# Every second block inverse of a chunked recurrence worked out on GpSimd

## The chip, the cores and the metric

The kernel runs on one core of a Trainium2 chip. A core has five engines, which take their own instructions in order and wait for each other by semaphores: TensorE (PE, matrix products; its weight loads are listed as PEld), VectorE (DVE), ScalarE (ACT), GpSimd (POOL) and SyncE (SP, which here only issues DMAs). DMAs are issued by SP and by POOL, from the same in-order queues as the other instructions of these engines. The metric is the device time of one launch in microseconds (us).

## The reference

Two parts follow each other. The first is a recurrence with a 40 x 40 state for each of 4 x 8 heads over 768 steps; the second a two-layer MLP on its output.

```python
for t in range(S):                                   # S = 768
    y[:, :, t] = np.einsum('bhd,bhde->bhe', rt, state)
    Sa = np.einsum('bhde,bhe->bhd', state, at)
    state_decay = state * wt[:, :, None, :] - np.einsum('bhd,bhe->bhde', Sa, bt)
    state = state_decay + np.einsum('bhd,bhe->bhde', vt, kt)
...
x = attn_out.transpose(0, 2, 1, 3).reshape(B * S, H * D)   # 3072 x 320
h = x @ w_in                                         # 320 -> 2048
sp = np.where(h > 20.0, h, np.log1p(np.exp(np.minimum(h, 20.0))))
g = h * np.tanh(sp)
out = g @ w_out                                      # 2048 -> 320
```

## The kernel before

**The recurrence in chunks.** The 768 steps are cut into 12 chunks of 64, taken in six pairs. In a chunk, the steps act on each other through a strictly lower triangular matrix, and the inverse of identity plus that matrix turns 64 dependent steps into matrix products. For each chunk there are four pieces of work.

- `pre_a(c, be)` (L126 to L203, twice for each chunk): the loads of `wa` and `bk` on SP's queue; the running products P of the decays by scans on DVE (L145 to L157), of which the last columns are copied out at L150; `bk` scaled on DVE (L170); P stored to `pD` from POOL's queue (L172); products on PE (L186) that give the triangular blocks `GP` and the factor `HA`, evicted by ACT (L188 to L190) and DVE (L191, L193); a small memset on POOL (L198) and transposes on PE (L202) for `bkn`.
- `pre_inv(n)` (L205 to L221, once for each pair): all 32 x 32 diagonal blocks of the pair are inverted at once, one block in a partition. DVE transposes `GP` into the tile `XL` (L209) and sets its diagonal to one (L210). Then 30 steps of forward substitution: step i multiplies column i below the diagonal with the first i elements of row i into `tmp` (L214) and adds that to `XL` (L216). Both have (31-i)*i elements in a partition, 30 to 240. There is one buffer for `XL` and one for `tmp`, and each of the 60 operations needs the one before. L218 transposes `XL` into `TT`, L220 part of that into `T1` (kept in `GP`'s tile).
- `post_inv(n)` (L223 to L260): PE multiplies with `TT` (L232), ACT evicts (L235), PE multiplies with `T1` (L241), ACT gathers the blocks of the 64 x 64 inverse in `bdT` (L249 to L251), and PE forms with them and `HA` the matrix `KT` of each chunk of the pair (L258, evicted at L260).
- `step(c)`: what hangs on the state. PE multiplies `KT` with `VS` (L284), evicted into `UVT` (L286), transposed (L293) into `UVQ`, multiplied with `bdr` (L314, masked on DVE at L316), and L334 and L339 give the output, which ACT evicts into `yev` (L343), and the next state, which DVE makes (L342, L346) and PE transposes (L304). The loads of the next chunk into `VS` (L267), `UVT` (L270) and `bdr` (L271), single buffers each, and the store of `yev` to `yD` (L370) stand on POOL's queue.

The loop over pairs goes: step 2n, `pre_a` of pair n+2, inverse of pair n+1, step 2n+1. The inverses n = 1, 3 and 5 are those of the second, fourth and sixth pair; steps 2, 6 and 10 need them.

**The MLP.** The weights come as 64-bit values and are turned into two float32 parts in pieces of 512 columns. A piece takes a DMA (`cv_d`, on SP's queue), an ACT operation (L459), three on DVE (L461 to L463), one on ACT (L494) and one on DVE (L495), with single buffers for most of the pieces. They are issued beside the last pairs of the recurrence. The matmuls of the first layer (L585) and the second (L605 to L607) follow; they read `yD` and `pD` back.

**What sets the order.** The code is written in loops; a scheduler orders the instructions of each engine by priorities, to which a table of offsets (`OFF`) adds for each part. What stands first in an engine's queue is waited for.

Of the kernel before, what the change touches and what calls it, by code (L numbers as in the profile page):

```python
# [10 lines left out]
ALU = mybir.AluOpType  # L11
# [67 lines left out]
def attention(ctx, tc, I, yD, pD, nch, M):  # L79
    nc = tc.nc  # L80
    V, A, PE, SP, G = nc.vector, nc.scalar, nc.tensor, nc.sync, nc.gpsimd
# [123 lines left out]
    def pre_inv(n):  # L205
        gp = GP[n]

        X = iw.tile([128, 32, 32], F32, name="XL", bufs=NXL)
        V.transpose(X.rearrange("p t j -> p j t"), gp[:, :, 1].rearrange("p u j -> p j u"))  # L209
        V.memset(X.rearrange("p t j -> p (t j)")[:, 0:1024:33], 1.0)  # L210
        for i in range(1, 31):
            tmp = iw.tile([128, 240], F32, name="tmp", bufs=NTMP)
            tv = tmp[:, 0:(31 - i) * i].rearrange("p (t j) -> p t j", j=i)
            V.tensor_tensor(out=tv, in0=X[:, i + 1:32, i:i + 1].broadcast_to([128, 31 - i, i]),  # L214
                            in1=X[:, i:i + 1, 0:i].broadcast_to([128, 31 - i, i]), op=ALU.mult)
            V.tensor_tensor(out=X[:, i + 1:32, 0:i], in0=X[:, i + 1:32, 0:i], in1=tv, op=ALU.add)  # L216
        TT = iw.tile([128, 32, 32], F32, name="TT", bufs=NTT)
        V.transpose(TT.rearrange("p u t -> p t u"), X)  # L218
        T1 = gp[0:64, :, 0]
        V.transpose(T1, TT[0:64])  # L220
        return TT, T1  # L221
# [159 lines left out]
    def inv(n):  # L381
        with at(tc, 'I%d' % n), at(tc, 'I'):
            TT, T1 = pre_inv(n)
        with at(tc, 'J%d' % n):
            post_inv(n, TT, T1)
# [274 lines left out]
```

## Time and profile before

| | |
|---|---|
| median of 3 runs | 845.22 us (842.81 to 847.49) |
| the profiled execution | 842.54 us |
| its span in the profile | 840.7 us |
| recurrence, up to about | 470 us |
| PE busy over the span | 737.5 us (88%) |
| DVE busy | 463.3 us (55%) |
| ACT busy | 427.9 us (51%) |
| POOL busy | 103.3 us (12%) |
| DMA | 61.92 MB, 74 GB/s over the span |

The busy rows average over stages. The profile also cuts the span in 40 slices of 21 us; each digit is the busy share in tenths:

```profile
PE   2545898998989889888749999999999999999998
...
DVE  6789889659879758947962649221222222122110
ACT  4533657774665766676457646333333333333331
POOL 8100021132123023211210200000000000000000
PEclk9755699899999999999978999999999999999999
```

For the first 22 slices PE, DVE and ACT share the work of the recurrence; behind them PE is full. POOL does little but issue DMAs after its memsets at the start. What lies around the span in the execution is 1.84 us.

### The profile page before, as it was taken

Reading aid. Unit: us, or ns where it says so; the run is one execution under the profiler, and the core shown is the slowest. Engines: PE = TensorE matmul, PEld = TensorE weight load, DVE = VectorE, ACT = ScalarE, POOL = GpSimd, SP = SyncE. Lnnn points to the kernel's source line nnn. Section 1 sums busy time; section 2 is a strip of 40 time slices with the busy share of each in tenths; the row PEclk is TensorE's granted clock in tenths of the full one; section 3 lists DMA queues with packets and bytes.
Section 4 is the critical chain, followed back from the end, with each engine's and each line's share of the span. In section 5 each row is a group of like instructions: output and inputs, shape, how many; then the busy total and the mean of one; then the engine's idle time right before and its main releaser. Section 6 shows DMA issues by size and latency. Waiting matters only on the chain.

```text
span 840.7 us, 18817 instructions
## 1 busy us (share of the span) xinstructions
PE 737.5 (88%) x7816; PEld 688.5 (82%) x7816; DVE 463.3 (55%) x975; ACT 427.9 (51%) x937; POOL 103.3 (12%) x182
## 2 busy tenths in 40 slices
PE   2545898998989889888749999999999999999998
PEld 2444687887778778777648899999999999999998
DVE  6789889659879758947962649221222222122110
ACT  4533657774665766676457646333333333333331
POOL 8100021132123023211210200000000000000000
PEclk9755699899999999999978999999999999999999
DMA  6422232333333133313543744211120121100000
GB/s 173 139 72 64 82 78 67 96 75 94 89 96 88 57 86 98 96 26 98 139 123 82 186 132 127 54 39 32 38 54 29 26 54 36 35 20 16 16 1 32
DMA packets 58213, 61.92 MB, mean 74 GB/s; under 512 B 25536, under 2 KB 48704, under 8 KB 58128
## 3 DMA queue, kind: packets, MB, share of 16 engines
q1 hardware_dynamic: 49296, 40.94, 17.4%
q0 software_dynamic: 8832, 19.79, 9.4%
q8 instruction: 61, 1.00, 0.5%
q14 instruction: 24, 0.20, 0.1%
HBM read 48.79 MB, written 11.86 MB: 72 GB/s over the span
## 4 chain that ended last, share of the span: by engine, by line
PE 61%; ACT 15%; DVE 15%; DMA 5%; issue 4%; SPq 0%; POOL 0%; ACTq 0%; DVEq 0%
PE ph L585 20%; PE po L605 7%; PE po L606 7%; PE po L607 6%; PE pa L186 4%; PE pa L258 3%; PE pq L314 3%; PE pq L334 2%; DMA cv_d<-in_wi 2%; DVE XL L216 2%; DVE tmp L214 2%; ACT KT L260 2%; ACT bdT L250 1%; ACT bdT L249 1%; ACT ad L155 1%
## 5 line engine op out<-in xcount | busy, mean ns | idle before, releaser
L585 PE MATMUL ph<-xh,w_ih 128*128 128x256 f32 x576 | 148.9, 283 | 0.0
L587 ACT ACTIVATE g<-ph 128x512 f32<-128x512 f32 x96 | 57.3, 598 | 179.7 <-PE ph L585 179.7
L591 DVE TENSOR_TENSOR gl<-g,gh 128x1024 fp32r<-128x1024 f32 x48 | 58.6, 1224 | 160.3 <-ACT gh L590 160.0
L585 PE MATMUL ph<-xh,w_il 128*128 128x256 f32 x576 | 123.7, 283 | 0.0
L186 PE MATMUL pa<-bk,ad 128*128 128x168 f32 x384 | 85.5, 372 | 42.2 <-DVE bk L170 15.0
L606 PE MATMUL po<-w_ol,gh 128*128 128x320 f32 x384 | 118.6, 309 | 0.0
L607 PE MATMUL po<-w_oh,gl 128*128 128x320 f32 x384 | 118.3, 309 | 0.0
L605 PE MATMUL po<-w_oh,gh 128*128 128x320 f32 x384 | 117.8, 309 | 0.1
L585 PEld LDWEIGHTS ph<-xh,w_ih 128*128 128x128 f32 x576 | 109.5, 190 | 0.2 <-issue 0.2
L186 PEld LDWEIGHTS pa<-bk,ad 128*128 128x128 f32 x384 | 70.4, 232 | 47.6 <-issue 23.1
L585 PE MATMUL ph<-xl,w_ih 128*128 128x256 f32 x384 | 100.7, 284 | 0.0
L585 PEld LDWEIGHTS ph<-xh,w_il 128*128 128x128 f32 x576 | 96.2, 190 | 0.1
L585 PEld LDWEIGHTS ph<-xl,w_ih 128*128 128x128 f32 x384 | 73.1, 190 | 0.2 <-issue 0.2
L605 PEld LDWEIGHTS po<-w_oh,gh 128*128 128x128 f32 x384 | 71.8, 188 | 0.6 <-ACT w_oh L494 0.5
L606 PEld LDWEIGHTS po<-w_ol,gh 128*128 128x128 f32 x384 | 72.1, 188 | 0.2 <-DVE w_ol L495 0.2
L607 PEld LDWEIGHTS po<-w_oh,gl 128*128 128x128 f32 x384 | 72.1, 188 | 0.0
L216 DVE TENSOR_TENSOR XL<-XL,tmp 128x30 f32<-128x30 f32 (+9 forms) x180 | 58.8, 326 | 2.6
L214 DVE TENSOR_TENSOR tmp<-XL 128x30 f32<-128x30 f32 (+9 forms) x180 | 58.2, 323 | 2.6
L314 PE MATMUL pq<-bdr,UVT 128*128 128x128 f32 x384 | 55.2, 288 | 4.6 <-DVE UVQ L316 3.8
L258 PE MATMUL pa<-bdT,HA 128*104 128x128 f32 x384 | 52.7, 289 | 7.1 <-ACT bdT L251 4.8
L258 PEld LDWEIGHTS pa<-bdT,HA 128*104 128x104 f32 x384 | 47.2, 181 | 10.3 <-ACT bdT L251 5.9
L314 PEld LDWEIGHTS pq<-bdr,UVT 128*128 128x128 f32 x384 | 48.6, 197 | 7.0 <-DVE UVQ L316 4.9
(89 smaller groups left out, 1237.3 us busy)
## 6 DMA issues: line engine op xcount, KB each, us to landing
wa<-in_wa SPq DMA_DIRECT2D x48, 162.5 KB
bk<-in_bk SPq DMA_DIRECT2D x48, 160.0 KB
cv_d<-in_wi SPq DMA_DIRECT2D x12, 512.0 KB
cv_d<-in_wo SPq DMA_DIRECT2D x8, 640.0 KB
pD<-P POOLq DMA_DIRECT2D x48, 81.2 KB, 2.4
VS<-in_vN POOLq DMA_DIRECT2D x24, 160.0 KB, 3.3
UVT<-in_vD POOLq DMA_DIRECT2D x24, 160.0 KB, 4.0
bdr<-in_rD POOLq DMA_DIRECT2D x24, 160.0 KB, 4.5
```

The lines of the kernel that those rows point to most:

```text
L186: PE.matmul(pt[:, j], ad[:, s0 + j].rearrange("p k a t -> p (k a t)"), bk[:, s0 + j], start=(j == 0), stop=True, skip_group_check=True)
L214: V.tensor_tensor(out=tv, in0=X[:, i + 1:32, i:i + 1].broadcast_to([128, 31 - i, i]), in1=X[:, i:i + 1, 0:i].broadcast_to([128, 31 - i, i] ...
L216: V.tensor_tensor(out=X[:, i + 1:32, 0:i], in0=X[:, i + 1:32, 0:i], in1=tv, op=ALU.add)
L258: PE.matmul(pk[:, j], ha[:, s0 + j], bd[:, s0 + j].rearrange("p a t -> p (a t)"), start=(j == 0), stop=True, skip_group_check=True)
L260: A.copy(kt[:, s0:s0 + 4], pk)
L314: PE.matmul(pq[:, s], UVT[:, g * 4 + s, be * 128:be * 128 + 128], br[:, be, g * 4 + s].rearrange("p a t -> p (a t)"), start=(s == 0), stop ...
L585: PE.matmul(o, w, x, start=(j == 0 and n == 0), stop=(n == 7), skip_group_check=True)
L587: A.activation(g[:, f0:f0 + 2], ph, AF.Mish)
L591: V.tensor_tensor(out=gl, in0=g, in1=gh.bitcast(F32), op=ALU.subtract)
L605: PE.matmul(po[k], gh[:, j, t], oh, start=(f == 0), stop=False, skip_group_check=True)
L606: PE.matmul(po[k], gh[:, j, t], ol, start=False, stop=False, skip_group_check=True)
L607: PE.matmul(po[k], gl[:, j, t], oh, start=False, stop=(f == 15), skip_group_check=True)
```

## The change

The two operations of the substitution are issued on GpSimd for odd n and stay on VectorE for even n. Their operands and order in the code stay, and so do the transposes and the memset around them, on VectorE.

```diff
         V.memset(X.rearrange("p t j -> p (t j)")[:, 0:1024:33], 1.0)
+
+        D = G if n % 2 else V
         for i in range(1, 31):
             tmp = iw.tile([128, 240], F32, name="tmp", bufs=NTMP)
             tv = tmp[:, 0:(31 - i) * i].rearrange("p (t j) -> p t j", j=i)
-            V.tensor_tensor(out=tv, in0=X[:, i + 1:32, i:i + 1].broadcast_to([128, 31 - i, i]),
+            D.tensor_tensor(out=tv, in0=X[:, i + 1:32, i:i + 1].broadcast_to([128, 31 - i, i]),
                             in1=X[:, i:i + 1, 0:i].broadcast_to([128, 31 - i, i]), op=ALU.mult)
-            V.tensor_tensor(out=X[:, i + 1:32, 0:i], in0=X[:, i + 1:32, 0:i], in1=tv, op=ALU.add)
+            D.tensor_tensor(out=X[:, i + 1:32, 0:i], in0=X[:, i + 1:32, 0:i], in1=tv, op=ALU.add)
```

Behind the two added lines every line number is higher by 2: L214, L216, L218, L220, L232 become L216, L218, L220, L222, L234, and so on.

The scheduler places the moved operations among POOL's other instructions. At the sixth pair (n = 5) POOL's queue held only the loads and stores of the steps; `yev_5164` is the output of step 9, and the rows behind are the loads for step 11. Before:

```order
L270 DMA UVT_118<-in_vD 40x8x128 x2
L271 DMA bdr0_121<-in_rD 40x16x64 x2
L370 DMA yD_57<-yev_5164 40x1024 x2
L267 DMA VS0_116<-in_vN 64x2x320
L267 DMA VS1_117<-in_vN 64x2x320
```

In the changed kernel the operations of this inverse (`XL_4746`) stand on both sides of that store:

```order
L216 TENSOR_TENSOR tmp_4788<-XL_4746 128x238
L218 TENSOR_TENSOR XL_4746<-XL_4746,tmp_4788 128x17x14
L273 DMA bdr0_121<-in_rD 40x16x64 x2
L372 DMA yD_57<-yev_5164 40x1024 x2
L216 TENSOR_TENSOR tmp_4791<-XL_4746 128x240
L218 TENSOR_TENSOR XL_4746<-XL_4746,tmp_4791 128x16x15
L216 TENSOR_TENSOR tmp_4794<-XL_4746 128x240
```

Of its 60 operations 28 stand ahead of the store and 32 behind it, from i = 15 on. On DVE, at the same place, the transposes into `TT_4839` and `T1` (written as `GP_3855`) stood right behind the last operation but one conversion:

```order
L214 TENSOR_TENSOR tmp_4836<-XL_4746 128x30
L216 TENSOR_TENSOR XL_4746<-XL_4746,tmp_4836 128x30
L495 SCALAR_TENSOR_TENSOR w_il2_5097<-cv_w_5118,w_ih2_5096 128x512
L218 STREAM_TRANSPOSE TT_4839<-XL_4746 128x32x32
L220 STREAM_TRANSPOSE GP_3855<-TT_4839 64x32x32
```

Now two further pieces of the weights (`cv_w_5130`, `cv_w_5140`) stand ahead of them, and the first operation of a third between the two:

```order
L463 TENSOR_SCALAR cv_w_5140<-cv_m_5143 128x512
L464 SCALAR_TENSOR_TENSOR cv_w_5140<-cv_m_5143,cv_w_5140 128x512
L465 SCALAR_TENSOR_TENSOR cv_w_5140<-cv_d_5141,cv_w_5140 128x512
L497 SCALAR_TENSOR_TENSOR w_il3_5129<-cv_w_5140,w_ih3_5128 128x512
L220 STREAM_TRANSPOSE TT_4839<-XL_4746 128x32x32
L463 TENSOR_SCALAR cv_w_5150<-cv_m_5153 128x512
L222 STREAM_TRANSPOSE GP_3855<-TT_4839 64x32x32
```

At the fourth pair (n = 3, `TT_3264`) the order on PE changed. Before, the first matmuls on TT came in the middle of `pre_a` of chunk 8 (`pa_3012` to `pa_3038`), ahead of the transposes of `UVT` (`pu_3512`):

```order
L186 MATMUL pa_3012<-bk1_99,ad1_101 128x168 x3
L186 MATMUL pa_3020<-bk1_99,ad1_101 128x168 x3
L314 MATMUL pq_3506<-bdr0_121,UVT_118 128x128 x2
L232 MATMUL pa_3267<-TT_3264,GP_2037 32x32 x20
L186 MATMUL pa_3028<-bk1_99,ad1_101 128x168
L232 MATMUL pa_3267<-TT_3264,GP_2037 32x32
```

In the changed kernel they stand behind the rest of that, the transposes and the first products of the next `pre_a` (`pa_3069`, `pa_3077`):

```order
L316 MATMUL pq_3506<-bdr0_121,UVT_118 128x128 x4
L295 MATMUL pu_3512<-cst_95,UVT_118 128x128 x3
L202 MATMUL pa_3044<-cst_95,bk1_99 128x128 x4
L295 MATMUL pu_3512<-cst_95,UVT_118 128x128
L295 MATMUL pu_3518<-cst_95,UVT_118 128x128 x4
L306 MATMUL pu_3525<-cst_95,ST0_122 128x128 x4
L186 MATMUL pa_3069<-bk0_98,ad0_100 128x168 x3
L186 MATMUL pa_3077<-bk0_98,ad0_100 128x168 x3
L286 MATMUL pu_3533<-KT_2538,VS0_116 64x64 x8
L286 MATMUL pu_3533<-KT_2557,VS1_117 64x64
L234 MATMUL pa_3267<-TT_3264,GP_2037 32x32 x6
```

Eight L186, eight L202, eight L295 and a few others moved ahead of TT's first reader. At the second pair (n = 1) the operations stand among the stores and loads of steps 0 and 1; the last 20 of them stand behind a store of P (`P_1293`, L172), and 16 matmuls of L286 that stood ahead of L234 on PE now stand behind it.

## The prediction

> **What bounds the kernel now.** I read the page first: the span, the chain that ended last, and the groups of the two lines that the change touches.
>
> ```profile
> span 840.7 us, 18817 instructions
> ...
> PE 61%; ACT 15%; DVE 15%; DMA 5%; issue 4%; SPq 0%; POOL 0%; ACTq 0%; DVEq 0%
> ...
> L216 DVE TENSOR_TENSOR XL<-XL,tmp 128x30 f32<-128x30 f32 (+9 forms) x180 | 58.8, 326 | 2.6
> L214 DVE TENSOR_TENSOR tmp<-XL 128x30 f32<-128x30 f32 (+9 forms) x180 | 58.2, 323 | 2.6
> ```
>
> PE carries 61% of the chain, DVE 15%. Each of the two lines runs 30 times for each of six inverses. The idle time ahead of them is 2.6 us in 180: each follows the one before. What three inverses cost must be read from the stages in which they stand, so next I cut the span into windows, one around each moved inverse (from its first transpose, L209, to its first reader on PE, L232), the stretch behind the last, and the MLP. Columns: window, length, then busy time (count) of PE, weight loads, DVE, ACT, POOL, the granted PE clock, DMA share, GB/s.
>
> ```profile
> 100.50:147.80 47.30, 42.68 (x594) 38.17 (x594) 42.46 (x110) 32.22 (x83) 9.07 (x17) 0.95 0.32 78
> 243.60:282.00 38.40, 33.68 (x495) 30.02 (x495) 35.92 (x98) 24.95 (x62) 8.14 (x15) 1.00 0.29 80
> 383.50:432.50 49.00, 33.53 (x516) 29.65 (x516) 44.56 (x116) 25.05 (x55) 13.96 (x21) 0.97 0.52 143
> ...
> 500.00:825.00 325.00, 324.90 (x2468) 324.26 (x2467) 90.09 (x97) 125.12 (x179) 0.00 (x0) 1.00 0.15 43
> ```
>
> DVE is busy 90%, 94% and 91% of the three windows, so it looks like the bound there; but PE is also at 90% and 88% in the first two. From 500 on PE is full (324.90 of 325), so what comes late to the MLP ends late. An inverse is 30 x (0.326 + 0.323) = 19.5 us by the groups' means, with (31-i)*i elements in step i, 165 in the mean and 9920 in all. Last, who waits for the result: PE's waits on TT in the first, second and third window, and the rows of its transpose and of the first matmul on it.
>
> ```profile
> PE pa L232 <- DVE TT L218: 0.2, 1, 0.2
> ...
> PE pa L232 <- DVE TT L218: 0.7, 1, 0.7
> ...
> PE pa L232 <- DVE TT L218: 7.3, 1, 7.3
> ...
> 145.75 1.98 DVE L218 STREAM_TRANSPOSE TT<-XL 128x1024 f32<-128x1024 f32 x1
> 280.00 1.94 DVE L218 STREAM_TRANSPOSE TT<-XL 128x1024 f32<-128x1024 f32 x1
> 430.51 1.89 DVE L218 STREAM_TRANSPOSE TT<-XL 128x1024 f32<-128x1024 f32 x1
> ...
> 147.79 0.44 PE L232 MATMUL pa<-TT,GP 32*32 32x32 f32 x16 [0.16 <-DVE TT L218]
> 282.00 0.82 PE L232 MATMUL pa<-TT,GP 32*32 32x32 f32 x40 [0.72 <-DVE TT L218]
> 432.46 1.92 PE L232 MATMUL pa<-TT,GP 32*32 32x32 f32 x64 [7.28 <-DVE TT L218]
> ```
>
> The first two inverses arrive when PE gets to them; the third is already what PE waits for, 7.3 us, and behind it PE has nothing of the MLP to do yet. **So an inverse that comes later costs its lateness, nearly in full, in all three places; one that comes earlier gains at most these 8.2 us and what a freer DVE gives elsewhere.** The question is whether POOL ends them later.
>
> **What is removed.** 180 operations leave DVE: 3 x 19.5 = 58.5 us of its time. The chain of waits followed back in 139-148, 243-284 and 383-434 puts the two lines at 15.3%, 14.1% and 13.9%:
>
> ```profile
> by line: DVE TT L218 22.1%; DVE UVQ L316 14.1%; DVE wa L157 12.8%; DVE bk L170 12.6%; DVE XL L216 9.5%; DVE HA L191 8.3%; DVE tmp L214 5.8%; ACT bdT L249 4.5%; DVE GP L193 3.7%; ACT GP L189 3.6%; ACT HA L190 3.0%; issue 2.3%
> ...
> by line: issue 7.7%; DVE tmp L214 7.2%; DVE XL L216 6.9%; ACT KT L260 6.2%; DVE UVQ L316 6.1%; DVE P L147 6.0%; DVE wa L157 5.8%; DVE XL L209 5.1%; DVE TT L218 4.8%; DVE wa L152 4.2%; ACT bdT L251 3.6%; ACT ad L155 3.3%; DVE bk L170 3.0%; A
> ...
> by line: DMA cv_d<-in_wi 33.3%; DVE XL L216 7.4%; ACT cv_m L459 6.6%; DVE tmp L214 6.5%; DVE cv_w L463 6.0%; issue 5.7%; DVE cv_w L461 5.4%; PE pq L314 4.6%; DVE cv_w L462 4.3%; DVE UVQ L316 4.2%; DVE XL L209 4.0%; DVE TT L218 3.6%; DVE w_i
> ```
>
> That is 1.4 + 5.8 + 7.1 = 14 us that could go if POOL cost nothing. Besides, DVE's other work (P scans, UVQ, ST) is done sooner; PE's idle time in the first two windows is 4.6 and 4.7 us (length less busy), and the waits in it are mostly for ACT. I count **-2 us**.
>
> **What is added: the price of an operation on POOL.** No row shows POOL with two inputs. What it shows:
>
> ```profile
> L110 POOL MEMSET bk<- 128x1344 f32 x2 | 2.4, 1217 | 0.3 <-POOLq L649 0.3
> ...
> L649 POOL MEMSET const-float32-0.0<- 128x1 f32 x1 | 0.1, 98 | 0.2 <-issue 0.2
> ...
> L271 POOL DMA_DIRECT2D bdr<-in_rD x24 | 20.4, 855 | 26.2 <-PE pq L339 13.4 <-issue 12.7
> ...
> 410.09 0.40 DVE L216 TENSOR_TENSOR XL<-XL,tmp 128x234 f32<-128x234 f32 x1
> 410.53 0.40 DVE L214 TENSOR_TENSOR tmp<-XL 128x228 f32<-128x228 f32 x1
> ```
>
> A memset costs 0.098 us fixed and (1217-98)/1343 = 0.83 ns an element for one write. The cheapest case is that the reads are hidden: 0.098 + 165 x 0.83 ns = 0.24 us, less than on DVE; the dearest row of a POOL instruction is 0.855 us. If each of two reads and one write takes a pass at the memset's pace, an operation has 0.098 + 165 x 2.5 ns = 0.51, and with the 0.04 us that DVE shows between dependent operations (410.09 + 0.40 to 410.53) some 0.05 more: **0.56 us**. I take this, as it counts each access at a pace that is measured on this engine, and keep 0.24 and 0.855 as the ends. An inverse is then 60 x 0.148 + 9920 x 2.5 ns = 33.7 us, against 19.5.
>
> The Trainium skill ("GPSIMD Engine Reference", section 3.1) gives a tensor_tensor of 2048 elements as 4497 ns on GpSimd against 2293 ns on VectorE, 1.96 times; as an estimate by that page an inverse takes 38 us, and the sum would be some 10 us more. No run here shows it yet.
>
> **POOL's queue is the other half.** It issues the loads and stores of each step in order, so an operation behind such a row waits for what that row waits for. Rows of POOL and DVE:
>
> ```profile
> 137.54 1.02 POOL L172 DMA_DIRECT2D pD<-P  x2 [9.51 <-DVE w L150]
> 278.58 1.02 POOL L172 DMA_DIRECT2D pD<-P  x2 [8.88 <-DVE w L150]
> 427.24 1.09 POOL L370 DMA_DIRECT2D yD<-yev  x2
> ...
> 102.79 0.16 DVE L214 TENSOR_TENSOR tmp<-XL 128x30 f32<-128x30 f32 x1
> 243.58 2.16 DVE L209 STREAM_TRANSPOSE XL<-GP 128x1024 f32<-128x1024 f32 x1
> ```
>
> Inverse 1 (second pair) starts at 102.7. At POOL's pace: 33.7 + 9.1 us that POOL has in this window already + 2.0 for the transpose = 147.5. But 20 operations with 2640 elements (9.6 us) stand behind a pD store, which goes out at 137.5 in the trace: 137.5 + 1.0 + 9.6 + 2.0 = 150.1. With DVE freer that store comes earlier, so I take the middle, 148.8, 1.1 us behind the 147.7 of before; and some 0.9 us of PE work (L284) now stands behind TT instead of ahead of it. **+2 us.**
>
> Inverse 3 starts at 243.58 + 2.16: 245.7 + 33.7 + 9.8 (the window's 8.14 on POOL and 1.7 of a yD and a pD that went out just ahead and now stand behind the first operations) + 1.9 = 291.1, or with the store at 278.6, 23 operations and 3308 elements behind it (11.7 us), 293.3. Against 282.0 this is 9.1 to 11.3 late. In the changed order PE has work ahead of TT that stood behind it:
>
> ```profile
> 278.86 1.96 PE L186 MATMUL pa<-bk,ad 128*128 128x168 f32 x12
> ...
> 276.60 0.66 PE L202 MATMUL pa<-cst,bk 128*128 128x128 f32 x4 [1.25 <-ACT bkn L203]
> ...
> 115.36 1.04 PE L293 MATMUL pu<-cst,UVT 128*128 128x128 f32 x8
> ```
>
> By these rows eight L186 of two passes are 2.6, eight L202 some 1.2, eight L293 1.0, and the others (L304, L314, L284) 1.6: 6.4 us of cover. **+4 us** (2.7 to 4.9). Without that cover it is +10.
>
> Inverse 5 is the worst placed. In POOL's order 32 of its operations (5440 elements, 32 x 0.148 + 13.6 = 18.3 us) stand behind step 9's yD store, the last thing that step does, at 427.24 to 428.33 in the trace. The step itself becomes quicker, as XL operations no longer stand between its DVE work and the weight conversions; I give it 2.5 us. So 425.9 + 18.3 + 1.9 = 446.1 against 432.4: 13.7 late. On DVE two weight conversions now stand ahead of TT that came behind it; the second ended at 446.02 + 0.63 + 0.69 before and moves up too, so POOL decides, if narrowly. What is saved are the conversions' pieces on ACT in the chain behind TT:
>
> ```profile
> 433.70 0.66 ACT L459 ACTIVATE cv_m<-cv_d 128x512 f32<-128x512 f32 x1
> ...
> 446.02 0.63 ACT L494 ACTIVATE w_ih<-cv_w 128x512 fp32r<-128x512 f32 x1
> ```
>
> Five such pieces between 433 and 450, about 3 us, go into the idle time ahead. **+11 us.**
>
> Sum: -2 + 2 + 4 + 11 = **+15 us** on the profiled run's 842.54 (span 840.7 and 1.84 around it), **857.5**; the median of the runs, 845.22, lies 2.7 above the profiled one and inside their spread, so I don't shift it. The step loads that stand between the operations (VS, UVT, bdr) get up to 8 us late in inverse 1:
>
> ```profile
> 121.68 0.76 POOL L270 DMA_DIRECT2D UVT<-in_vD  x1 [2.94 <-PE pq L314]
> ...
> 135.90 0.94 PE L314 MATMUL pq<-bdr,UVT 128*128 128x128 f32 x6
> ```
>
> PE reads what they bring 14 us after the issue, so 6 us are left for the landing; I take that as enough. That cover is gone with dearer operations.
>
> **How the sum moves with the price.** Each 0.1 us is 6 us for inverse 1 and for 3, and 3.2 for 5: 15 us together. At 0.48 us the first two are hidden, and it is +6; at 0.3 only inverse 5's tail is left, which the -2 about pays; at 0.68, +33; at 0.8, +51.
>
> **Rivals.** *POOL is as quick as DVE* (under about 0.3 us an operation), and DVE was the bound of the three windows. For it: DVE's 90% and more, and the memset's 0.83 ns. Then TT of the second comes when PE wants it, and inverse 5's tail of 32 operations takes under 9.6 us behind yD: 425.9 + 9.6 + 1.9 = 437.4 against 432.4, less 3 on ACT, less the 2 elsewhere: 842.5; at 0.24 us, 840.6. Up to 14 us (828) only if the tail did not stand behind that store, which the order excludes. **Faster needs both a price near the low end and more relief than I count: 8%.** *Cheap enough to hide* (0.3 to 0.45): 842 to 847, 13%. *Dear operations* (0.8 and more: a hand-over or a start on POOL that a memset without inputs does not show): +50, 893, 15%.
>
> *The two engines block each other.* DVE runs many operations with two inputs from SBUF in the same windows:
>
> ```profile
> L157 DVE TENSOR_TENSOR_SCAN wa<-wa,d 128x519 f32<-128x519 f32 x24 | 29.6, 1233 | 6.8 <-ACT ad L155 6.7
> L170 DVE TENSOR_TENSOR bk<-bk,wa 128x1024 f32<-128x1024 f32 x24 | 29.1, 1212 | 1.4 <-DMA bk<-in_bk 1.3
> L462 DVE SCALAR_TENSOR_TENSOR cv_w<-cv_m,cv_w 128x512 int32<-128x512 int32 x12 | 8.2, 686 | 0.2
> ```
>
> If POOL stood still for each of them, half of DVE's other time in the first two windows (42.5 - 19.5 = 23 us) would delay each of these inverses by about 10, and two conversions of three such operations (6 x 0.69) the tail of the last by 4 to 5: +25 on my sum, **882**. Before, POOL hardly ran beside DVE, so nothing in the trace speaks for or against: 14%. This is a rule of the Trainium skill ("SBUF — State Buffer", section "SBUF: two separate sides"): GpSimd and VectorE share a pair of ports under an exclusive lock, and a DVE operation with two SBUF inputs and a GpSimd operation that reads SBUF block each other. No run here shows it yet.
>
> **How the numbers follow.** Forecast 50% (price 0.48 to 0.68: 849 to 875), blocking 14%, dear 15%, hidden 13%, faster 8%. The range leaves out the fast case and the far part of the dear one: 843 to 895. A measurement of this kernel can tell about 0.5%, 4.2 us. Faster by more than that 0.08; within it 0.12, nearly all of the hidden case; slower 0.80.
>
> **What would show it.** Right: POOL's 180 rows at 0.5 to 0.6 us; PE's wait for TT at inverse 5 near 20 us, with the releaser's chain through POOL from yD; inverses 1 and 3 a few us late; the MLP unchanged but later. Wrong: a POOL mean under 0.35 or over 0.8; TT of inverse 5 released by a conversion and not by POOL; PE idle in step 1 for UVT or bdr; DVE's two-input rows longer than 1.2 and 0.7 us where POOL runs beside them.

## The result, and the profile after

The changed kernel takes **883.38 us** (median of 4 runs, 879.99 to 887.40) against 844.27 us before (4 runs): ratio 1.0452, 95% interval 1.040 to 1.050, so **39 us slower**. The profiled execution took 886.25 us, its span 884.5. The forecast was +15 us, 857.5, in a range of 843 to 895: the way and the range held, the size did not.

The page of the changed kernel, the lines that answer to those of before:

```profile
span 884.5 us, 18828 instructions
...
PE 58%; DVE 13%; ACT 12%; POOL 9%; issue 5%; DMA 2%; ACTq 0%; DVEq 0%; POOLq 0%; SPq 0%
...
L218 POOL TENSOR_TENSOR XL<-XL,tmp 128x30 f32<-128x30 f32 (+14 forms) x90 | 59.8, 664 | 6.2
...
L216 POOL TENSOR_TENSOR tmp<-XL 128x30 f32<-128x30 f32 (+14 forms) x90 | 51.6, 573 | 28.3 <-DVE XL L209 22.6
```

The 180 operations take 0.62 us in the mean on POOL against 0.32 on DVE, and POOL, 0% of the chain before, has 9% of it. The same windows as before, each from an inverse's first transpose to its first reader on PE, then the MLP (columns as before):

```profile
100.20:156.00 55.80, 46.70 (x561) 42.83 (x561) 28.64 (x49) 31.50 (x81) 45.70 (x76) 0.84 0.29 70
253.80:310.00 56.20, 41.13 (x553) 36.82 (x554) 32.10 (x51) 33.29 (x84) 47.34 (x79) 0.91 0.30 76
402.70:477.80 75.10, 38.34 (x516) 35.16 (x516) 39.22 (x64) 28.63 (x60) 50.93 (x81) 0.76 0.38 108
540.00:865.00 325.00, 324.92 (x2469) 324.26 (x2468) 90.61 (x96) 124.04 (x178) 0.00 (x0) 1.00 0.16 43
```

They were 47.3, 38.4 and 49.0 us long and are 55.8, 56.2 and 75.1: 8.5, 17.8 and 26.1 more. The MLP costs what it did (324.92 of 325 us busy, 324.90 before). DVE fell from 90, 94 and 91% to 51, 57 and 52% of them. PE's waits for TT in the three windows, and its first matmul on it:

```profile
PE pa L234 <- DVE TT L220: 3.6, 1, 3.6
...
PE pa L234 <- DVE TT L220: 2.7, 1, 2.7
...
PE pa L234 <- DVE TT L220: 26.4, 1, 26.4
...
477.75 1.92 PE L234 MATMUL pa<-TT,GP 32*32 32x32 f32 x64 [26.42 <-DVE TT L220]
```

0.2, 0.7 and 7.3 us became 3.6, 2.7 and 26.4. That is not yet the whole of it, since PE is held up elsewhere too. POOL's timeline of the sixth pair's inverse (start, length, operation, what ended the idle time ahead of it) shows where 71 us go:

```profile
412.32 0.41 POOL L218 TENSOR_TENSOR XL<-XL,tmp 128x108 f32<-128x108 f32 x1
423.66 1.52 POOL L272 DMA_DIRECT2D UVT<-in_vD  x2 [10.92 <-PE pq L316]
425.19 0.46 POOL L216 TENSOR_TENSOR tmp<-XL 128x130 f32<-128x130 f32 x1
...
432.40 1.73 POOL L273 DMA_DIRECT2D bdr<-in_rD  x2
434.12 1.10 POOL L372 DMA_DIRECT2D yD<-yev  x2
435.98 1.24 POOL L269 DMA_DIRECT2D VS<-in_vN  x2 [0.75 <-PE pu L286]
...
443.18 1.52 POOL L272 DMA_DIRECT2D UVT<-in_vD  x2 [3.93 <-PE pq L316]
...
453.69 1.09 POOL L372 DMA_DIRECT2D yD<-yev  x2
454.81 0.62 POOL L216 TENSOR_TENSOR tmp<-XL 128x240 f32<-128x240 f32 x1
...
475.50 0.25 POOL L218 TENSOR_TENSOR XL<-XL,tmp 128x30 f32<-128x30 f32 x1
```

The chain stands still for 10.9 and 3.9 us at loads of UVT, which wait until PE has read the single buffer (L316). Behind step 9's store, at 453.7, 32 operations remain, and they take 20.9 us.

Put together for each inverse from its first operation on POOL to its last, by adding up such rows ("alone" is the sum of 0.20 us + 1.85 ns an element for L216 and 0.21 + 1.90 for L218, read off rows with nothing beside them):

| chain | total | 60 operations alone | more beside DVE | gaps of some 0.07 | issues between | waits at issues |
|---|---|---|---|---|---|---|
| predicted (1; 3) | 43; 44 | 30.7 | 0 | 3.0 | 9.1; 9.8 | 0 |
| changed kernel, n = 1 | 51.6 | 30.9 | 6.3 | 3.8 | 8.9 | 1.7 |
| changed kernel, n = 3 | 51.8 | 30.9 | 6.5 | 2.4 | 10.3 | 1.7 |
| changed kernel, n = 5 | 70.8 | 30.9 | 5.9 | 3.3 | 15.1 | 15.6 |

### The profile page after: what moved, and what is told of

It reads as the page before. It is cut to its first block, busy times and chain, and to the rows that moved or that the text cites. A ratio compares the mean times of both kernels' runs of the same rounds, so it can differ in the third digit from the quotient of the medians.

```text
span 884.5 us, 18828 instructions
## 1 busy us (share of the span) xinstructions
PE 749.4 (85%) x7816; PEld 701.9 (79%) x7816; DVE 428.1 (48%) x795; ACT 428.4 (48%) x937; POOL 214.4 (24%) x362
## 4 chain that ended last, share of the span: by engine, by line
PE 58%; DVE 13%; ACT 12%; POOL 9%; issue 5%; DMA 2%; ACTq 0%; DVEq 0%; POOLq 0%; SPq 0%
PE ph L587 20%; PE po L608 6%; PE po L607 6%; PE po L609 6%; PE pa L186 5%; POOL XL L218 4%; POOL tmp L216 4%; PE pa L260 3%; PE pq L316 3%; PE pq L336 2%; DVE XL L218 2%; DVE tmp L216 1%; PE pu L295 1%; DVE P L147 1%; PE pa L243 1%
## 5 line engine op out<-in xcount | busy, mean ns | idle before, releaser
L186 PE MATMUL pa<-bk,ad 128*128 128x168 f32 x384 | 89.0, 385 | 45.4 <-DVE bk L170 16.7
L186 PEld LDWEIGHTS pa<-bk,ad 128*128 128x128 f32 x384 | 73.9, 242 | 51.0 <-issue 24.9
L316 PE MATMUL pq<-bdr,UVT 128*128 128x128 f32 x384 | 54.8, 292 | 13.0 <-issue 7.8
L316 PEld LDWEIGHTS pq<-bdr,UVT 128*128 128x128 f32 x384 | 50.0, 204 | 14.4 <-issue 8.0
L218 POOL TENSOR_TENSOR XL<-XL,tmp 128x30 f32<-128x30 f32 (+14 forms) x90 | 59.8, 664 | 6.2
L260 PE MATMUL pa<-bdT,HA 128*104 128x128 f32 x384 | 56.4, 302 | 5.0 <-ACT bdT L253 4.2
L216 POOL TENSOR_TENSOR tmp<-XL 128x30 f32<-128x30 f32 (+14 forms) x90 | 51.6, 573 | 28.3 <-DVE XL L209 22.6
L260 PEld LDWEIGHTS pa<-bdT,HA 128*104 128x104 f32 x384 | 50.5, 191 | 8.0 <-ACT bdT L253 5.3
```

Of the source, the lines that this page charges most:

```text
L186: PE.matmul(pt[:, j], ad[:, s0 + j].rearrange("p k a t -> p (k a t)"), bk[:, s0 + j], start=(j == 0), stop=True, skip_group_check=True)
L216: D.tensor_tensor(out=tv, in0=X[:, i + 1:32, i:i + 1].broadcast_to([128, 31 - i, i]), in1=X[:, i:i + 1, 0:i].broadcast_to([128, 31 - i, i] ...
L218: D.tensor_tensor(out=X[:, i + 1:32, 0:i], in0=X[:, i + 1:32, 0:i], in1=tv, op=ALU.add)
L260: PE.matmul(pk[:, j], ha[:, s0 + j], bd[:, s0 + j].rearrange("p a t -> p (a t)"), start=(j == 0), stop=True, skip_group_check=True)
L316: PE.matmul(pq[:, s], UVT[:, g * 4 + s, be * 128:be * 128 + 128], br[:, be, g * 4 + s].rearrange("p a t -> p (a t)"), start=(s == 0), stop ...
```

## The experiments

**Each place alone.** The line that chooses the engine, for n = 5, n = 1 and n = 3 in turn:

```diff
-        D = G if n % 2 else V
+        D = G if n == 5 else V
```

> Only the sixth pair's inverse on GpSimd, the other two on VectorE. In the changed kernel the stage of this inverse got 24.6 us longer (from the transpose ahead of it to the end). If the three places add up: 844 + 25 = 869 us. If its loss was partly handed on from the two earlier ones: under 860. My prediction's term was 11: 855.

> Only the second pair's inverse on GpSimd. In the changed kernel the transpose ahead of the fourth pair's inverse came 10.3 us later than before. If the places add up: 854 us. My prediction's term was 2: 846.

> Only the fourth pair's inverse on GpSimd. If the three places add up to the whole change (39 us, of which the sixth pair alone showed 29.5 and the second 7): 2 to 3 us, 848. If the stage's own lateness in the changed kernel is what counts (9 us from the transpose ahead of it to the one ahead of the sixth pair): 854. My prediction's term was 4: 849.

Measured: 875.47 us for n = 5 (ratio to before 1.0354, 1.029 to 1.042), 853.00 for n = 1 (1.0097, 1.006 to 1.013) and 872.80 for n = 3 (1.0296, 1.023 to 1.036), that is +29.5, +7.0 and +26.6 on the medians of the runs beside them (30, 8 and 25 by the ratios). They do not add up to 39, and n = 3 alone costs some three times the highest of what was expected of it. POOL's timeline of that run shows where its chain lost time. The scheduler placed its operations anew, and two of the places are behind stores of P (L172), whose P is not there yet:

```profile
259.38 0.55 POOL L172 DMA_DIRECT2D pD<-P  x1 [9.92 <-DVE w L150]
...
279.39 0.53 POOL L172 DMA_DIRECT2D pD<-P  x1 [7.30 <-DVE w L150]
```

This chain took 76.6 us, 18.2 of them in waits and 17.9 in issues, where the same inverse took 51.8 in the changed kernel. So the cost of a place is not a property of the place alone; it goes with what the order puts between its operations.

**POOL's queue without loads and stores, everywhere.** All step loads and stores on SP's queue:

```diff
-QS = "SGGG"
+QS = "SSSS"
```

> The kernel before, with the step loads, the yD stores and the pD stores issued from SP's queue and not from POOL's; the inverses all on DVE. It is the control for the next run: all theories expect within 10 us of the 844 of before, as POOL's queue was never full; whatever it is, the next run is compared with it.

> The changed kernel with the same loads and stores on SP's queue, so that POOL's queue holds the inverses' operations and small memsets alone. Theory Q (the loss comes from the shared in-order queue: operations behind stores, step loads behind operations): an inverse takes 60 x 0.565 us and some 6 us beside DVE, 40 us, and all three end within 7 us of when PE wants them; the time is within 6 us of the control's. Theory P (the loss is the operations' own price, and their blocking by DVE): a chain of 40 us where DVE needs 45 with its other work would still be late as in the changed kernel, 20 to 39 us above the control.

The control took 867.98 us, 22 over the kernel before and not within 10 as expected, so the loads and stores are worse off on SP's queue. The changed kernel with it took 928.05, 60 more than its control. Both theories had that wrong. The chains did become short, 39.8, 34.9 and 37.4 us. The middle one, with nearly nothing of DVE beside it, gives the price free of everything else, first and last operation:

```profile
276.50 0.25 POOL L216 TENSOR_TENSOR tmp<-XL 128x30 f32<-128x30 f32 x1 [19.90 <-DVE XL L209]
...
311.12 0.25 POOL L218 TENSOR_TENSOR XL<-XL,tmp 128x30 f32<-128x30 f32 x1
```

34.9 us from 276.50 to 311.37, where I had 33.7. But DVE stood idle ahead of each TT, in its own in-order queue:

```profile
143.82 1.90 DVE L220 STREAM_TRANSPOSE TT<-XL 128x1024 f32<-128x1024 f32 x1 [17.57 <-POOL XL L218]
311.40 1.90 DVE L220 STREAM_TRANSPOSE TT<-XL 128x1024 f32<-128x1024 f32 x1 [19.82 <-POOL XL L218]
485.66 1.90 DVE L220 STREAM_TRANSPOSE TT<-XL 128x1024 f32<-128x1024 f32 x1 [21.80 <-POOL XL L218]
```

The three sum to 59.2 us, as much as the cost, and PE too is busy for only 7.5 us of them. TT stands in DVE's queue where a shorter chain would end, and all of DVE's later work is behind it. A free queue for POOL was of no use here, since another engine's queue waited in order for its result.

**The same for the sixth pair alone, with the order ahead of it untouched.**

```diff
     def step_loads(c):
+        SQ = SP if c >= 9 else G
...
-            OQ.dma_start(out=yD[c, be], in_=...)
+            (SP if c >= 8 else G).dma_start(out=yD[c, be], in_=...)
```

> The kernel before, with the loads for steps 9 to 11 and the yD stores of steps 8 to 11 issued from SP's queue; everything up to there is untouched. Control for the next run; SP's queue has the weight loads in that stage, so it may differ from the kernel before by 10 us either way.

> The same with the sixth pair's inverse on GpSimd: POOL's queue then holds its 60 operations in one piece, with no load or store between. Theory Q (the stage is long because of the 15 us of issues and 16 to 18 us of waits that stand between the operations in POOL's queue): the chain takes 36 to 42 us instead of 71, ends at 42 us from the first transpose (47 before), and the cost against the control is under 5 us instead of 29.5. Theory R (what costs is that VectorE's and PE's queues were ordered for a quicker chain, so they wait for it in order, wherever POOL's time goes): the chain is short as well, but the cost stays at 10 us or more, as VectorE's idle time ahead of TT.

The control took 851.90 us (ratio to the kernel before 1.0025, 0.998 to 1.007), with n = 5 on POOL 859.89 (1.013, 1.008 to 1.018): **8 to 9 us instead of 29.5**. The chain took 43.7 us instead of 71.6, of which 36.0 are operations and 2.8 issues. TT was there 47.8 us after L209 began (388.51), as good as before (48.9). So some 21 of the 29.5 us come from loads and stores in the same queue, as theory Q has it. Its 5 us were too few and its chain of 36 to 42 us too short. Ahead of TT, where theory R looked for the rest, DVE stood idle for 5.1 us, but PE waited for TT hardly longer than in the control. More of the rest shows at UVQ and UVT, in PE's waits of that stage:

```profile
PE pq L317 <- DVE UVQ L319: 8.9, 1, 8.9
PE pu L296 <- ACT UVT L289: 6.9, 4, 2.4
PE pa L234 <- DVE TT L220: 4.6, 1, 4.6
```

In its control these were 2.7, 2.8 and 3.5. Just behind that stage PE also waited 5.4 us for a load of bdr (0.9 in the control), which now goes out from SP's queue. The order behind the chain is new as well: step 9 ended 73.7 us after L209 began, and 43.7 in the control. So the 21 us are those of two orders, not of one with the queue alone changed.

**The weight conversions.** They moved up in DVE's queue, and in the run of n = 5 alone PE waited 8.5 us for a UVQ that stood behind one of them. First one load for nine pieces instead of nine loads, then no conversions at all beside the last pairs, with six copies in their place:

```diff
-            self.w_in(wp, cv, range(NQ0, NQ1))
+            d = cv.tile([128, CVW, 2], I32, name="cv_d")
+            self.tc.nc.sync.dma_start(out=d..., in_=self.I['wi'][:, 0:CVW]...)
+            self.w_in(wp, cv, range(NQ0, NQ1), d)
...
```

```diff
-            self.w_in(wp, cv, range(NQ0, NQ1))
...
+            for t in (h, l):
+                self.tc.nc.vector.tensor_copy(out=t, in_=self.ih[0])
```

> The kernel before, where the weight conversions beside the last pairs all read one loaded piece and the other eight loads are left out (the weights are wrong, so the output is not the reference's). Control for the next run. In the profile before, the load of a piece is 33% of the chain from 383 to 434; without it the sixth pair's stage should be some 5 to 15 us shorter: 831 to 841.

> The same with the sixth pair's inverse on GpSimd. Theory C (the conversions, which moved ahead of the steps' operations on VectorE, hold step 8 and 9 up at the pace of their loads, and so the yD store on which the rest of the inverse waits): without those loads, step 9's store comes 8 us or more sooner after the inverse's start than in the run of n = 5 alone (58.7 us), and the cost against the control falls from 29.5 to under 20 us. Theory T (the 60 operations' length and their places in POOL's queue alone): it stays at 25 to 32.

> The kernel before, with the weight conversions beside the last pairs left out and six copies in their place (the weights are wrong, so the output is not the reference's). Control for the next run. DVE, ACT and the loads are relieved in the sixth pair's stage: 825 to 840.

> The same with the sixth pair's inverse on GpSimd. POOL's order up to step 8 is that of the run with n = 5 alone. Theory C' (conversions that stand ahead of the steps' operations on VectorE make step 9's store late): step 9's store comes at most 45 us after the inverse's first transpose (58.7 with them), and the cost falls from 29.5 to under 20. Theory Q alone: the waits and issues in POOL's queue stay, and so does the cost, 25 or more.

Measured: 849.56 and 878.51, then 845.19 and 875.00 us. Against their controls n = 5 on POOL costs 29.0 and 29.8 us, as with the conversions. Both controls are as slow as the kernel before and not 5 to 20 us faster as expected, though 33% of the chain in that stage was put down to the loads of the pieces: taking them away gained nothing, so that share was no bound. So the conversions are not what makes the move dear. Without them the chain on POOL still took 69.1 us, 15.3 of issues and 17.4 of waits, and DVE stands idle for the last operation:

```profile
460.46 1.90 DVE L220 STREAM_TRANSPOSE TT<-XL 128x1024 f32<-128x1024 f32 x1 [20.58 <-POOL XL L218]
```

**Do the two engines block each other?** Three chains on a scratch tile during the MLP, where DVE does little but one kind of operation; then with that operation changed into a copy:

```diff
+        for i in list(range(1, 31)) * 3:
+            tv = zt[...]
+            G.tensor_tensor(out=tv, in0=zx[...], in1=zx[...], op=ALU.mult)
+            G.tensor_tensor(out=zx[...], in0=zx[...], in1=tv, op=ALU.add)
...
-            V.tensor_tensor(out=gl, in0=g, in1=gh.bitcast(F32), op=ALU.subtract)
+            V.tensor_copy(out=gl, in_=g)
```

> The kernel before with three more inverse chains (180 operations on a scratch tile) on GpSimd during the MLP, where POOL is empty and VectorE runs one kind of operation with two inputs from SBUF, 1024 elements in 1.22 us, every 6.8 us. Theory L (GpSimd and VectorE block each other when both read SBUF, VectorE twice): an operation takes 0.2 us + 1.85 ns an element alone, and up to 1.1 us more where such a VectorE operation runs; VectorE's 1.22 us get longer by up to 0.6. Theory 'no block, POOL's times scatter': no relation between the two. The total is unchanged by both, since PE is full there: 843 to 848.

> The same, but the VectorE operation in the MLP is a copy of g (one input; so the low part of the activations is wrong and the output is not the reference's). Theory L by number of inputs: no POOL operation is longer than alone by over 0.15 us where it runs. Theory 'any VectorE work slows POOL': the same excess per VectorE microsecond as with two inputs.

With two inputs, POOL's rows around one such operation of DVE, and that operation:

```profile
585.89 0.51 POOL L619 TENSOR_TENSOR zt<-zx 128x184 f32<-128x184 f32 x1
586.48 1.41 POOL L621 TENSOR_TENSOR zx<-zx,zt 128x184 f32<-128x184 f32 x1
587.96 0.48 POOL L619 TENSOR_TENSOR zt<-zx 128x168 f32<-128x168 f32 x1
...
585.98 1.50 DVE L591 TENSOR_TENSOR gl<-g,gh 128x1024 fp32r<-128x1024 f32 x1 [6.04 <-ACT gh L590]
```

An addition of 184 elements takes 0.56 alone and 1.41 here; it ends 0.41 after DVE's operation does (587.89 against 587.48). DVE's own, started while POOL was at work, took 1.50 instead of 1.22. The 180 operations took 28.5 us more than alone, and none of the rows without DVE beside them did. With the copy:

```profile
608.62 0.91 POOL L619 TENSOR_TENSOR zt<-zx 128x220 f32<-128x220 f32 x1
...
608.29 0.81 DVE L591 CAST gl<-g 128x1024 fp32r<-128x1024 f32 x1 [5.96 <-ACT g L587]
```

0.61 became 0.91: a one-input copy blocks as well, for its shorter length, so the theory by the number of inputs falls in that form. In both, POOL's operation ends some 0.4 us after DVE's, and 0.4 is what its elements alone take (184 and 220 at 1.9 ns are 0.35 and 0.42). The changed kernel shows the same; its rows, and DVE's at that time:

```profile
146.45 0.55 POOL L218 TENSOR_TENSOR XL<-XL,tmp 128x168 f32<-128x168 f32 x1
147.60 1.31 POOL L218 TENSOR_TENSOR XL<-XL,tmp 128x150 f32<-128x150 f32 x1
...
147.41 1.24 DVE L157 TENSOR_TENSOR_SCAN wa<-wa,d 128x519 f32<-128x519 f32 x1 [0.38 <-ACT ad L155]
```

All its operations that took over 0.12 us more than alone (37 of 180) ran beside a DVE operation with two inputs from SBUF; DVE's operations that read PSUM (L191, L318, L344) lengthened none by themselves. The block is there as the Trainium skill has it ("SBUF — State Buffer", section "SBUF: two separate sides": an exclusive lock, taken by a DVE operation in a two-port mode or with two SBUF inputs). That the copy ran in such a mode is not shown here. The block is 6 us of each chain. The totals were single runs, 853.09 and 847.36, inside the spread of the runs before beside them (842.67 to 853.98).

**What could be gained at all.** The 60 operations of n = 1, 3 and 5 left out:

```diff
-        for i in range(1, 31):
+        for i in range(1, 31) if n % 2 == 0 else ():
```

> The kernel before with the 60 operations of the inverses n = 1, 3 and 5 left out (so the output is not the reference's). It bounds what taking them off VectorE can give at all. Theory 'DVE is the bound of the three stages': 58.5 us of its work are gone and 30 or more of the time, 814 or less. My prediction's reading (the first two inverses arrive when PE wants them, the third is waited for 7.3 us, 14 us of these operations stand on the chain): 8 to 14 us, 831 to 837.

838.26 us (ratio 0.9872, 0.979 to 0.995): 8 us on the medians, 11 by the ratio (4 to 18), for 58.5 us of DVE's time. DVE at 90% was busy, not the bound.

**More time for the chain.** The operations issued an iteration earlier, the transposes into TT where they were:

```diff
-ORDER = '0aiA1'
+ORDER = '0aiA1x'
...
+            elif k == 'x':
+                if n + 2 < nds:
+                    inva(n + 2)
```

> The changed kernel with the 60 operations issued a whole iteration earlier: right after the pre-work of their pair and behind step 2n+1, while the transposes into TT and T1 stay where they were. GpSimd then has two steps of time for a chain of 40 to 50 us. Theory T (lateness is all: the chain is longer than the time that it is given): the 39 us go, and the time is within 8 us of the kernel before or up to 8 below it (what leaving the operations out gives). Theory B (blocking of VectorE and the queue's waits cost as much wherever the chain stands): 860 or more.

> The same with the inverses of the second to the sixth pair all on GpSimd, so that 97 us leave VectorE. Theory T: equal to the run before or up to 8 us less, if each chain ends within its iteration. Theory B: some 15 us more than the run before, as 6 us of blocking come with each chain.

880.22 us (ratio 1.041, 1.035 to 1.046), and with five inverses on POOL 899.00 (1.063), 18.8 more. It did not test what it was meant to. The transpose that starts the fourth pair's chain ran at 246.5 us, where the changed kernel has 253.9 and the kernel before 243.6, so the chains started no earlier than in the kernel before. Their input GP comes no sooner: its last write (L193) ended at 246.4, just ahead of that transpose. Whether a chain with a real head start would cost nothing stays open.

## Why the prediction was right in its direction and wrong in its size

- **Term by term.** In the profiled executions the spans differ by 43.8 us (the medians by 39). The first transpose (L209) of the second, fourth and sixth pair moved from 100.5, 243.6 and 383.5 to 100.2, 253.8 and 402.7, the first matmul on the sixth pair's TT from 432.5 to 477.8. So the three places cost 10.5, 9.0 and 26.1 us, where the sum had 2, 4 and 11, and the rest gave back 1.8, where it had 2.
- **The step that failed most is in inverse 5: "The step itself becomes quicker, as XL operations no longer stand between its DVE work and the weight conversions; I give it 2.5 us."** That 32 operations stand behind step 9's store was right. But the store came 51.0 us after L209 began instead of 43.7, so 7.3 later and not 2.5 earlier, and the operations behind it took 20.9 us instead of 18.3. These two make up the miss: TT was forecast 13.7 us late and was 26.1. Step 9 itself ended 6 us later (its last `yev` 49.5 us after L209 began instead of 43.5), and the rest of the 7.3 is POOL's own work ahead of the store. No row of that stage shows PE waiting for a load. The windows show 38.34 us for its 516 matmuls instead of 33.53, at a lower granted clock, and it waited longer for UVT and UVQ, before:

```profile
PE pu L293 <- ACT UVT L286: 3.3, 3, 1.1
PE pq L314 <- DVE UVQ L316: 2.6, 2, 1.4
...
PE pq L334 <- DVE UVQ L316: 0.5, 1, 0.5
```

  and after:

```profile
PE pu L295 <- ACT UVT L288: 4.0, 3, 2.3
PE pq L316 <- DVE UVQ L318: 3.7, 2, 3.3
PE pq L336 <- DVE UVQ L318: 2.0, 1, 2.0
```

  Why these waits grew is not settled; leaving out the conversions did not lower the cost. What the chain lost by standing in one queue with the step's loads and stores is: of 29.5 us for this place alone, some 21 went with them. For the 8 that stay no run gives the cause.
- **The price of an operation held in its sum, and partly by luck.** 33.7 us were forecast for 60 operations, 34.9 were measured with nothing beside them. The parts are off both ways: what does not depend on the size, with the gaps, is some 17 us (60 x (0.205 + 0.075)) where 9 were counted, and the elements take 18.6 where 24.8 were counted, so the idea of three passes at the memset's pace is not borne out. The Trainium skill's ratio of 1.96 ("GPSIMD Engine Reference", section 3.1), which is for 2048 elements, is more than these sizes show alone: 0.635 against 0.40 us at 240 elements, 1.6 times. The prediction also calls 0.855 us the dearest row of POOL; the memset beside it has 1.217.
- **"DVE was the bound" was rightly a rival with little weight.** Leaving the work out gives 8 to 11 us, within the 8 to 14 that the chain of waits allowed.
- **The blocking was a rival and not a term; it belonged in the sum.** Each chain got 6 us longer, where the rival had 10, 10 and 5. That is most of inverse 1's miss: TT was forecast 1.1 us late and was 8.2 late, and this place alone costs 7.0 us, not 2. That the rival's time, 882, is so near to the measured 883 is luck, since its three delays are not the measured ones. DVE's operations were held as well (L147 took up to 1.64 us, before at most 1.24), which the prediction had named as a sign of being wrong.
- **"So 6 us are left for the landing; I take that as enough" failed too.** It was checked for inverse 1 only, with loads up to 8 us late. There the second load of UVT went out at 135.14 instead of 123.29, 12 us later, and PE waited 1.2 us for it. In inverse 3 PE had read bdr for the last time by 276.3 (L341), but the second load for step 5 went out only at 289.36, behind POOL's operations; it landed at 295.28, and the L316 that reads it started at 295.48:

```profile
289.36 0.86 POOL L273 DMA_DIRECT2D bdr<-in_rD  x1
...
295.48 0.77 PE L316 MATMUL pq<-bdr,UVT 128*128 128x128 f32 x2 [7.82 <-issue]
```

  Before, both loads went out as soon as PE had read the buffer, and were there long before the reader:

```profile
266.94 1.69 POOL L271 DMA_DIRECT2D bdr<-in_rD  x2 [0.52 <-PE pq L339]
...
277.10 0.94 PE L314 MATMUL pq<-bdr,UVT 128*128 128x128 f32 x6
```

  PE stood for 7.8 us. The row names no releaser; that it was the load is read from the landing 0.2 us ahead of it.
- **The cover of inverse 3 fits the totals.** TT was 17.7 us later after L209 than before, and the next inverse's transpose 9.0 us: 8.7 us did not arrive there, against 6.4 counted. That the place's 9 us are so near to its 4 hangs on the order: alone it costs 26.6.
- **What the sum left out.** It had no term for PE's clock: PE's busy time rose by 11.9 us for the same matmuls. How much of this is in the 43.8 was not measured. That the places don't add (7 + 27 + 30 alone) goes with the order, which was new in each kernel: inverse 3's chain took 51.8 us in one and 76.6 in another.

## What to carry to other kernels

Before work goes to an engine that also issues DMAs, list what its in-order queue holds between the operations: each issue is a wait in the chain, and each operation delays every load behind it, which a step ahead then waits for. Price the chain by its operations alone, then by these two, and add what the other engine's reads block; here the first came out within 4%, and the rest was where the forecast failed. Don't credit a step with being quicker because an engine is freer: here it got slower. And ask first what leaving the work out would give: some 8 to 11 us were to be had, against operations that take 34.9 us where they took 19.5.

## What the runs showed of the hardware that was not expected

- A DVE operation with two inputs from SBUF, or a copy in SBUF, holds a GpSimd operation that reads SBUF until its own end, and GpSimd's operation then still takes about the time of its elements: the three shown end 0.26 us later with 150 elements, 0.41 with 184 and 0.43 with 220. It costs 0.85 us beside a DVE operation of 1.22 us and 0.30 beside a copy of 0.7.
- PE's granted clock was lower in the windows in which PE waited more: 0.84, 0.91 and 0.76 in the three windows, which had 0.95, 1.00 and 0.97 before, and PE's busy time rose from 737.5 to 749.4 us for the same 7816 matmuls. Its share in the 39 us was not measured by itself.
